# The last rows of w_out on other lanes, and two scalars loaded earlier, in a decode step with attention and a gated MLP

## The chip, the core and the metric

The kernel runs on one core of a Trainium2 chip. A core has five engines that run side by side, each with its own instruction stream: PE (matrix products), DVE (vector operations), ACT (activations and copies), POOL (general small work) and SP, which in this kernel only issues transfers. Sixteen DMA engines move data between device memory and the core's on-chip memory of 128 lanes (partitions). Transfers are issued here from SP and ACT. One transfer is cut into packets, which the DMA engines work off; after its last packet of a transfer each engine reports with a small completion packet of 4 bytes.

The metric is the device time of one execution, in microseconds (us); the median of several runs is taken.

## The reference

One decode step for four sequences: x is 4 x 640 in bf16. The layer norm of x feeds two branches, which are added to x.

```python
def _A_ref(x, k_cache, v_cache, wq, wo):
    B, Sq, D = x.shape                       # 4, 1, 640
    q = (x @ wq) as 32 heads of 128
    scores = einsum('bhqd,bhkd->bhqk', q, k_cache) * Dh ** (-0.5)    # 4096 keys
    o = einsum('bhqk,bhkd->bhqd', softmax(scores), v_cache)
    return o.reshape(B, Sq, Hq * Dh) @ wo

def _B_ref(x, w_in, w_sp, b_sp, w_out):
    z = gelu(x @ w_in)                       # 640 x 1728
    z1, z2 = z[..., :864], layernorm(z[..., 864:])
    g = w_sp * z2 + b_sp                     # w_sp is 1 x 1, b_sp one number
    return (z1 * g) @ w_out                  # 864 x 640

xn = layernorm(x)
return x + _A_ref(xn, ...) + _B_ref(xn, ...)
```

The K and V caches are 4 x 32 x 4096 x 128 in bf16, 134 MB each. With one query row for each head, every byte of them is used once, so nearly all of the 282 MB that the kernel reads are K and V.

## The kernel before

**Units.** The work is cut into 16 units, each of eight heads of one sequence. A unit's K is 4 MB, 128 lanes of 64 KB, and so is its V. K goes through a ring of seven places (`ring`), each a quarter of a unit; V has one whole place (`v_all`). For each quarter of K, DVE multiplies with the query (L537) and folds the halves (L543), and PE adds up the rest (L555). Then come row sums (L569), a maximum, the exponential on ACT (L596), a spreading of the probabilities over heads into `p_m` (L607), and the products with V on PE (L631). After each group of four units the result is multiplied by a part of `wo` (L699).

**Loads.** All large loads are issued by SP, in the order of the list `loads` (L195 to L203). `pump` (L207) goes through it and stops where a place is still taken. At the start stand `wq` (L118), the first quarter of K, the second, `load_w` (`w_in` at L127 and those parts of `w_out` that take one transfer), the other half of K, `load_w_few` (the part of `w_out` that takes several transfers), and unit 1's K. Each transfer reports to one of eight landing semaphores, taken in turn, and the issue that comes eight later on the same semaphore first waits for that landing.

**The MLP.** `w_in` and most of `w_out` lie in `v_all` before the first V comes, the last rows of `w_out` in `p_buf`, the room that later holds `p_m`. The 864 rows of `w_out` are split by `W_OUT` (L62) into parts of n lanes with r rows each. Part one has 128 lanes of five rows, part two 128 lanes of one row, part three 12 lanes of eight rows, 10240 bytes to a lane; part three goes by four transfers, of every fourth lane (three lanes each, L123). The generator `gmlp` (L397) does the products with `w_in` (L404, 14 column groups of the same parts), copies them out of PSUM once for each number of lanes (L414), and does gelu, layer norm and gate on DVE, ACT and PE. Its last step multiplies with `w_out` (L503). Only then is `v_all` free for the first V.

**The scalars.** `wsp_bf` and `bsp_bf`, one number each, are loaded from ACT's queue (L735, L736), after ACT's copy for the first unit's query (L527). POOL casts both to fp32 (L464, L466) for the gate.

**The end.** The last unit's V comes in two halves, the second cut into four transfers, and the last part of `wo` in six (L228, L231). After its last product (L699) ACT copies the sum (L823), and two transfers of 2.5 KB write the output.

Of the kernel before, what the change touches and what calls it, by code (L numbers as in the profile page):

```python
# [10 lines left out]
BF16 = mybir.dt.bfloat16  # L11
# [6 lines left out]
def kernel(  # L18
# [14 lines left out]
    nc = tc.nc  # L33
    P = nc.NUM_PARTITIONS
# [24 lines left out]
    RW = 8  # L59
    QW = HC * Dh  # L60
    RING = 2 * NK - 1
    W_OUT = ((P, 5, 1), (P, 1, 1), (12, 8, 4))  # L62
    assert sum(n * r for n, r, _ in W_OUT) == Fh
    NFC = sum(r for _, r, _ in W_OUT)

    def up(n):
        return -(-n // 256) * 256

    PW = sum(up(r * D) for _, r, _ in W_OUT[1:])
    NOH = D // 2  # L70
# [10 lines left out]
    const = ctx.enter_context(tc.tile_pool(name="const", bufs=1))  # L81
# [17 lines left out]
    ring = places.tile([P, RING, QW], BF16, name="k_ring")  # L99
    x_bf = ring[0:Bsz, 1, 0:D]  # L100
    nc.scalar.dma_start(out=x_bf, in_=A_x.flatten_outer_dims())
    v_all = places.tile([P, NK * QW], BF16, name="v_all")

    wq_sb = v_all[:, 0 : DC * HD].rearrange("p (c n) -> p c n", c=DC)
# [2 lines left out]

    at_v = up(DC * (HD + F))
    w_parts, f0, at_p = [], 0, 0
    for n, r, t in W_OUT:  # L110
        if f0 == 0:
            room = v_all[0:n, at_v : at_v + r * D]
        else:
            room = p_buf[0:n, at_p : at_p + r * D]
            at_p += up(r * D)
        w_parts.append((room.rearrange("p (k n) -> p k n", k=r), f0, n, r, t))
        f0 += n * r
    nc.sync.dma_start(out=wq_sb, in_=A_wq.rearrange("(p c) n -> p c n", c=DC))  # L118

    def load_part(part):  # L120
        w, f0, n, r, t = part
        rows = B_w_out[f0 : f0 + n * r].rearrange("(p k) n -> p k n", k=r)
        for l in range(t):  # L123
            nc.sync.dma_start(out=w[l:n:t], in_=rows[l:n:t])

    def load_w():
        nc.sync.dma_start(out=w_in_sb, in_=B_w_in.rearrange("(p c) n -> p c n", c=DC))  # L127
        for part in w_parts:
            if part[4] == 1:
                load_part(part)  # L130

    def load_w_few():
        for part in w_parts:
            if part[4] > 1:
                load_part(part)

    w_rows = [
# [105 lines left out]
    for e in range(PAR):  # L243
        nc.gpsimd.tensor_copy(
            out=of_row[:, e, :, :, e, :],
            in_=ident[:].rearrange("p (k q) -> p q k", q=QD)[:, 0:Bsz, :, None].to_broadcast(
                [P, Bsz, NQ, LN]
            ),
# [15 lines left out]
    for i in range(NSTAT):  # L264
# [5 lines left out]
        out=rstd[:], in_=mv[:, 1:2], func=ACT.Sqrt, bias=eps_tile[:Bsz], scale=1.0  # L270
# [4 lines left out]
        out=xn_bf,  # L275
# [4 lines left out]
        op1=ALU.mult,  # L280
    )

    wsp_bf = const.tile([1, 1], BF16)
    bsp_bf = const.tile([1, 1], BF16)

    xn_v = xn_bf.rearrange("b (p c) -> b c p", c=DC)
    xnT_ps = ps_m.tile([P, DC, Bsz], BF16, tag="m")
    for c in range(DC):
        nc.tensor.transpose(
            out=xnT_ps[:, c, :], in_=xn_v[:, c, :], identity=ident[:Bsz, :Bsz]  # L290
# [8 lines left out]
    for e in range(PAR):  # L299
        q_ps = ps_pv.tile([P, HG, Dh], FP32, tag="pv", name="q_ps")  # L300
        for c in range(DC):
            for k in range(NQ):
                nc.tensor.matmul(  # L303
                    out=q_ps[k * QD : (k + 1) * QD],
# [5 lines left out]
        rows = const.tile([P, HG, Dh], BF16, name=f"q_rows{e}")  # L310
        nc.vector.tensor_scalar(  # L311
            out=rows[:], in0=q_ps[:], scalar1=scale_qk, scalar2=None, op0=ALU.mult
# [7 lines left out]
        out=hot[:].rearrange("p c h -> p (c h)"),  # L320
        in_=ident[:].rearrange("p (g m) -> p m g", m=QD),
# [6 lines left out]
        out=pick[:, :, Bsz - 1 :].rearrange("p c (k q) -> p c k q", q=QD)[  # L328
            :, :, :, 0 : PAR * Bsz : Bsz
        ],  # L330
        in_=hot[:].rearrange("p c (k e) -> p c k e", e=PAR),
# [4 lines left out]
        out=of_set[:],  # L336
        in_=hot[:].rearrange("p c h -> p (c h)")[:, 0 : PAR * Bsz].rearrange(
            "p (e b) -> p e b", b=Bsz
        ),
# [5 lines left out]
    with nc.allow_low_precision("0 and 1"):  # L345
        nc.vector.tensor_reduce(
            out=own[:],
            in_=ident[:].rearrange("p (h l) -> p h l", h=HT),
# [5 lines left out]
        out=par[:], in_=own[:].rearrange("p (k e) -> p e k", e=PAR), axis=AX.X, op=ALU.add  # L354
# [3 lines left out]
        out=far[:],  # L358
# [13 lines left out]
    for half in range(2):  # L372
        nc.tensor.matmul(
            out=out_ps[OG * half : OG * half + OG, :],
# [15 lines left out]
    by_lanes = []  # L390
    for n, r, _ in W_OUT:
        if by_lanes and by_lanes[-1][0] == n:
# [122 lines left out]
    def stage_q(u):  # L515
        hg, b = divmod(u, Bsz)
        qb_ps = ps_m.tile([P, Dh], FP32, tag="m", name="qbc_ps")
        for e in range(PAR):
            nc.tensor.matmul(  # L519
                out=qb_ps[:],  # L520
                lhsT=of_row[:, e, b].rearrange("p k f l -> p (k f l)"),
                rhs=q_rows[e][:, hg, :],
                start=(e == 0),
                stop=(e == PAR - 1),
            )
        qbcs[u] = small.tile([P, Dh], BF16, name="qbc")
        nc.scalar.copy(out=qbcs[u][:], in_=qb_ps[:])  # L527
# [7 lines left out]
    def product(n):  # L535
        u, r, t = step(n)
        nc.vector.tensor_tensor(  # L537
            out=t, in0=t, in1=qbcs[u][:, None, :].to_broadcast([P, HC, Dh]), op=ALU.mult
        )
# [192 lines left out]
    E = mybir.EngineType  # L732
    with tc.manual_schedule(engines={E.PE, E.DVE, E.Activation, E.SP}):
        stage_q(0)
        nc.scalar.dma_start(out=wsp_bf[:], in_=B_w_sp[0:1, 0:1])  # L735
        nc.scalar.dma_start(out=bsp_bf[:], in_=B_b_sp[0:1].rearrange("(a b) -> a b", a=1))  # L736
        waiting = None
        mlp = gmlp()
        for n in range(NK * NU):
            u, i = divmod(n, NK)  # L740
            product(n)
            if n and n % 2 == 0:
                row_sums(n - 1)
            if i == 0 and u:
                head_max(u - 1)
                if waiting in taken:
                    picked(waiting)
            fold_half(n)
            if n == 1:
                next(mlp)  # L750
                next(mlp)
            if i == 0 and u:
                exps(u - 1)
                if waiting in pvs:
                    take(waiting)
                by_head(u - 1)
            sums(n)
            if i == 0 and u + 1 < NU:
                stage_q(u + 1)
            if i == 0 and waiting is not None:  # L760
                if waiting in taken:
                    picked(waiting)
                if waiting % Bsz == Bsz - 1:
                    group_turn(waiting // Bsz)
                    group_proj(waiting // Bsz)
                waiting = None
            if n == 0:
                next(mlp)
            if n == 1:
                next(mlp)  # L770
                next(mlp)
                next(mlp)
                busy.remove(V)
            if n in turns:
                w = waiting = turns[n]
                if w % Bsz == Bsz - 1:
                    group_den(w // Bsz)
                if w == NU - 3:
                    weighted(w, v_runs[:, 0:NC], more=True)
                    weighted(w, v_runs[:, NC:NR], NG // 2)  # L780
                else:
                    weighted(w, v_runs)
                if i < NK - 1:
                    take(w)
                busy.remove(V)
            pump()
        weighted(NU - 2, v_runs)
        row_sums(NK * NU - 1)
        head_max(NU - 1)
        exps(NU - 1)  # L790
        take(NU - 2)
        by_head(NU - 1)
        den = ps_m.tile([P, NQ, PAR, Bsz], FP32, tag="m", name="den_all")
        nc.tensor.matmul(
            out=den[:],
            lhsT=ones_sq[:],
            rhs=acc[(HG - 1) % NACC][:, :, 0 : PAR * Bsz],
            start=True,
            stop=True,
        )  # L800
        rden = small.tile([P, NQ, PAR, Bsz], FP32, name="rden_all")
        nc.vector.reciprocal(out=rden[:], in_=den[:])
        picked(NU - 2)
        u, b = NU - 1, Bsz - 1
        weighted(u, v_ends[0])
        take(u)
        pick_last(u, more=True)
        for c in range(NC):
            nc.tensor.matmul(  # L809
                out=o_last[0][:, :, :, b],  # L810
                lhsT=v_ends[1][:, c, :],
                rhs=p_m[:, u % 2, NG // 2 + c // CB, c % CB, :].rearrange("p (k e) -> p k e", e=PAR),
                start=False,
                stop=(c == NC - 1),
            )
        o_n = small.tile([P, NQ, PAR, Bsz], BF16, name="o_n_last")
        nc.vector.tensor_tensor(out=o_n[:], in0=o_last[0][:], in1=rden[:], op=ALU.mult)  # L817
        gr[HG - 1] = [o_n[:, h // PAR, h % PAR, :] for h in range(HT)]
        group_proj(HG - 1)

        res = v_all[:, 0:NOH]
        out_v = out.flatten_outer_dims()
        nc.scalar.copy(out=res[0 : OG + Bsz], in_=out_ps[0 : OG + Bsz])  # L823
        nc.scalar.dma_start(out=out_v[:, 0:NOH], in_=res[0:Bsz])
        nc.sync.dma_start(out=out_v[:, NOH:D], in_=res[OG : OG + Bsz])
# [30 lines left out]
```

## Time and profile before

| | |
|---|---|
| median of 3 runs | 661.95 us (661.85 to 662.0) |
| profiled execution | 662.09 us, its span 660.2 us |
| read from device memory | 282.24 MB, 428 GB/s over the span |
| busy in the span | DVE 522.6 us (79%), PE 317.0 us (48%), ACT 29.9 us, POOL 10.1 us |
| DMA, SP's queue (q1) | 8192 packets, 99.1% of the time of 16 engines |
| granted clock of PE | 0.692 |

The span goes from the first to the last instruction of the profiled execution; the rest of its time lies outside. A row of the page's slices has one digit for each fortieth of the span, the busy share in tenths. In a list of instruction groups stand line, engine, operation, shapes and number, then the busy time, the mean of one in ns, and the engine's idle time ahead of them with what ended it. The rows of a wait list have the time in all, the number of waits and the longest. The list of transfers gives the size of each and the median time from issue to landing. "SPq" and "ACTq" are an engine's instruction queue, where transfers are issued and waits are held.

### The profile page before, as it was taken

How to read it: one execution, taken by the hardware profiler on the slowest of the kernel's cores; microseconds unless marked ns; L12 is line 12 of the kernel's file. 1: busy time of each engine (PE TensorE's matmuls, PEld its weight loads, DVE VectorE, ACT ScalarE, POOL GpSimd, SP SyncE). 2: the span in 40 equal slices, each digit the busy share in tenths (PEclk: the TensorE clock that was granted, in tenths of full speed). 3: DMA queues.
4: the chain of work that ended last, by engine and by line, in shares of the span. 5: the costliest groups of instructions: out<-in, count | busy, mean ns of one | idle time of the engine just before them, and what ended most of it. 6: DMA issues, size and time to landing. Idle time of an engine off the chain costs nothing.

```text
span 660.2 us, 4777 instructions
## 1 busy us (share of the span) xinstructions
PE 317.0 (48%) x2083; PEld 136.3 (21%) x2083; DVE 522.6 (79%) x276; ACT 29.9 (5%) x73; POOL 10.1 (2%) x20
## 2 busy tenths in 40 slices
PE   0574372526427363452636336263452534737367
PEld 0231121212213121120212112121120211212124
DVE  1767978959597795969959598695969969999950
ACT  0020000000000000000000000000000000000000
POOL 2300000000000000000000000000000000000000
PEclk9757676766767676585767768676685867676785
DMA  9999999999999999999999999999999999999997
GB/s 369 433 461 434 417 441 434 433 437 438 421 445 426 437 430 441 437 422 433 434 441 441 418 437 441 430 441 421 434 441 437 426 421 445 422 427 436 449 409 284
DMA packets 8232, 282.55 MB, mean 428 GB/s; under 512 B 892, under 2 KB 2184, under 8 KB 2568
## 3 DMA queue, kind: packets, MB, share of 16 engines
q1 hardware_dynamic: 8192, 282.25, 99.1%
q8 instruction: 16, 0.26, 0.1%
q10 hardware_dynamic: 20, 0.01, 0.0%
q14 instruction: 4, 0.03, 0.0%
HBM read 282.24 MB, written 0.01 MB: 428 GB/s over the span
## 4 chain that ended last, share of the span: by engine, by line
DMA 62%; DVE 28%; PE 8%; issue 1%; ACT 0%; DVEq 0%
DMA k_ring<-in_A_k_cache_dram 53%; DVE k_ring L537 14%; DVE k_ring L543 7%; PE s_ps L555 6%; DMA v_all<-in_A_v_cache_dram 4%; DMA k_ring<-in_A_wo_dram 3%; DVE s_sb L569 3%; DMA v_all<-in_A_wq_dram 2%; DVE p_m L607 1%; DVE m L578 1%; PE q_ps L303 1%; PE pv L631 1%; PE out_ps L699 1%; DVE p_m L678 1%; DVE mf L580 1%
## 5 line engine op out<-in xcount | busy, mean ns | idle before, releaser
L537 DVE TENSOR_TENSOR k_ring<-k_ring,qbc 128x8192 bf16<-128x8192 bf16 x64 | 282.9, 4420 | 88.5 <-DMA k_ring<-in_A_k_cache_dram 87.9
L555 PE MATMUL s_ps<-k_ring,ident 128*128 128x512 bf16 x512 | 202.2, 566 | 313.8 <-DVE k_ring L543 313.7
L555 PEld LDWEIGHTS <-ident 128*128 128x128 bf16 x512 | 64.0, 130 | 430.0 <-issue 245.4
L543 DVE TENSOR_TENSOR k_ring<-k_ring 128x4096 bf16<-128x4096 bf16 x64 | 145.9, 2280 | 1.1
L631 PE MATMUL pv<-v_all,p_m 128*32 128x512 bf16 x960 | 62.5, 419 | 0.0
L569 DVE TENSOR_REDUCE s_sb<-s_ps 128x128 f32<-128x1024 f32 x32 | 39.0, 1218 | 3.7 <-PE s_ps L555 3.7
L607 DVE TENSOR_TENSOR p_m<-p_c,own 128x2048 bf16<-128x2048 bf16 x16 | 36.6, 2285 | 0.7 <-ACT p_c L596 0.7
L631 PEld LDWEIGHTS <-p_m 128*32 128x32 bf16 x992 | 26.6, 106 | 42.5 <-issue 23.3
L596 ACT ACTIVATE p_c<-s_sb,nm 128x256 bf16<-128x256 f32 x16 | 8.1, 508 | 342.9 <-DVE nm L588 342.9
L662 PEld LDWEIGHTS o_ps<-o_rows,pick 128*128 128x128 f32 x96 | 20.4, 294 | 4.3 <-issue 3.3
L662 PE MATMUL o_ps<-o_rows,pick 128*128 128x128 f32 x96 | 19.1, 367 | 0.0
L643 ACT COPY o_rows<-pv 128x512 f32<-128x512 f32 x16 | 9.4, 586 | 165.7 <-PE pv L631 165.7
L311 DVE TENSOR_SCALAR q_rows<-q_ps 128x512 bf16<-128x512 f32 x2 | 1.4, 692 | 12.8 <-PE q_ps L303 12.8
L817 DVE TENSOR_TENSOR o_n_last<-o_last,rden_all 128x32 bf16<-128x32 f32 x1 | 0.2, 192 | 12.2 <-PE o_last L809 12.2
L303 PE MATMUL q_ps<-v_all,xnT 128*32 128x512 bf16 x40 | 4.5, 630 | 9.3 <-DMA v_all<-in_A_wq_dram 9.3
L527 ACT CAST qbc<-qbc_ps 128x128 bf16<-128x128 f32 x16 | 4.3, 266 | 97.6 <-PE qbc_ps L519 97.6
L578 DVE TENSOR_REDUCE m<-s_sb 128x1 f32<-128x256 f32 x16 | 6.7, 420 | 0.5
L519 PE MATMUL qbc_ps<-q_rows,of_row 128*128 128x128 bf16 x32 | 6.0, 276 | 0.6 <-DVE q_rows L311 0.6
L519 PEld LDWEIGHTS <-of_row 128*128 128x128 bf16 x32 | 4.1, 132 | 8.1 <-issue 7.4
L716 PE MATMUL o_last<-hot,o_rows 128*128 128x8 f32 x32 | 4.9, 279 | 0.7 <-ACT o_rows L643 0.7
L716 PEld LDWEIGHTS o_last<-hot,o_rows 128*128 128x128 f32 x32 | 4.8, 226 | 1.8 <-ACT o_rows L643 1.6
L699 PE MATMUL out_ps<-k_ring,p_m 128*4 128x320 bf16 x48 | 4.0, 309 | 2.1 <-DVE p_m L691 2.1
(87 smaller groups left out, 81.4 us busy)
## 6 DMA issues: line engine op xcount, KB each, us to landing
k_ring<-in_A_k_cache_dram SPq DMA_DIRECT2D x5, 4096.0 KB, 27.2
v_all<-in_A_v_cache_dram SPq DMA_DIRECT2D x2, 4096.0 KB, 28.2
v_all<-in_A_wq_dram SPq DMA_DIRECT2D x1, 5120.0 KB, 15.4
k_ring<-in_A_k_cache_dram SPq DMA_DIRECT2D x2, 2048.0 KB
k_ring<-in_A_v_cache_dram SPq DMA_DIRECT2D x1, 4096.0 KB
k_ring<-in_A_wo_dram SPq DMA_DIRECT2D x3, 1280.0 KB, 20.6
v_all<-in_B_w_in_dram SPq DMA_DIRECT2D x1, 2160.0 KB
k_ring<-in_A_v_cache_dram SPq DMA_DIRECT2D x1, 2048.0 KB
```

Source lines behind the costliest of these rows:

```text
L303: nc.tensor.matmul(out=q_ps[k * QD : (k + 1) * QD], lhsT=xnT[:, c, :], rhs=wq_v[:, c, k, e], start=(c == 0), stop=(c == DC - 1),)
L519: nc.tensor.matmul(out=qb_ps[:], lhsT=of_row[:, e, b].rearrange("p k f l -> p (k f l)"), rhs=q_rows[e][:, hg, :], start=(e == 0), stop=(e ...
L537: nc.vector.tensor_tensor(out=t, in0=t, in1=qbcs[u][:, None, :].to_broadcast([P, HC, Dh]), op=ALU.mult)
L543: nc.vector.tensor_tensor(out=t[:, :, 0:HD2], in0=t[:, :, 0:HD2], in1=t[:, :, HD2:Dh], op=ALU.add)
L555: nc.tensor.matmul(out=s, lhsT=ident[:], rhs=t[:, :, g * RW : (g + 1) * RW], start=(g == 0), stop=(g == m - 1),)
L569: nc.vector.tensor_reduce(out=scores[u][:].rearrange("p (r c) -> p r c", r=NK)[:, lo : hi + 1 : hi - lo], in_=sums_ps.pop(n // 2)[:], axis ...
L578: nc.vector.tensor_reduce(out=m1[:], in_=scores[u][:], axis=AX.X, op=ALU.max)
L607: nc.vector.tensor_tensor(out=p_m[:, u % 2], in0=p_c.pop(u)[:].rearrange("p (g c) -> p g c", c=CB)[:, :, :, None].to_broadcast([P, NG, CB, HT]
L631: nc.tensor.matmul(out=pvs[u][cg * QD : (cg + 1) * QD, :], lhsT=p_m[:, u % 2, g0 + n].rearrange("p c h -> p (c h)"), rhs=v_at[:, n * CB : ...
L662: nc.tensor.matmul(out=gr[hg][:], lhsT=pick[:, c, Bsz - 1 - b : P + Bsz - 1 - b], rhs=o[:, c, :], start=(b == 0 and c == 0), stop=(b == Bs ...
L699: nc.tensor.matmul(out=out_sum(half), lhsT=o, rhs=wo_sb[:, n, half * NOH : (half + 1) * NOH], start=False, stop=(hg == HG - 1 and n == HT ...
L716: nc.tensor.matmul(out=o_last[0][:, :, :, u % Bsz], lhsT=o[:, c, :], rhs=hot[:, c, :].rearrange("p (k e) -> p k e", e=PAR), start=(c == 0) ...
```

## The change

`W_OUT` now says of each part which lanes go together in how many transfers. Part one is as before. Part two is 32 lanes of one row, in one transfer. Part three is 24 lanes of eight rows: the first 18 lanes by three transfers of every third lane (six lanes each), the last 6 by two transfers of every second lane (three lanes each). The number of column groups stays 14, and the bytes of `w_out` are the same. The loads of `wsp_bf` and `bsp_bf` stand right behind that of x, ahead of every other transfer of ACT.

```diff
-    W_OUT = ((P, 5, 1), (P, 1, 1), (12, 8, 4))
+    W_OUT = ((P, 5, ((P, 1),)), (32, 1, ((32, 1),)), (24, 8, ((18, 3), (6, 2))))
...
     nc.scalar.dma_start(out=x_bf, in_=A_x.flatten_outer_dims())
+    wsp_bf = const.tile([1, 1], BF16)
+    bsp_bf = const.tile([1, 1], BF16)
+    nc.scalar.dma_start(out=wsp_bf[:], in_=B_w_sp[0:1, 0:1])
+    nc.scalar.dma_start(out=bsp_bf[:], in_=B_b_sp[0:1].rearrange("(a b) -> a b", a=1))
...
     def load_part(part):
-        w, f0, n, r, t = part
+        w, f0, n, r, cuts = part
         rows = B_w_out[f0 : f0 + n * r].rearrange("(p k) n -> p k n", k=r)
-        for l in range(t):
-            nc.sync.dma_start(out=w[l:n:t], in_=rows[l:n:t])
+        l0 = 0
+        for lanes, t in cuts:
+            for l in range(l0, l0 + t):
+                nc.sync.dma_start(out=w[l : l0 + lanes : t], in_=rows[l : l0 + lanes : t])
+            l0 += lanes
...
         for part in w_parts:
-            if part[4] == 1:
+            if len(part[4]) == 1:
                 load_part(part)
...
         for part in w_parts:
-            if part[4] > 1:
+            if len(part[4]) > 1:
                 load_part(part)
...
     with tc.manual_schedule(engines={E.PE, E.DVE, E.Activation, E.SP}):
         stage_q(0)
-        nc.scalar.dma_start(out=wsp_bf[:], in_=B_w_sp[0:1, 0:1])
-        nc.scalar.dma_start(out=bsp_bf[:], in_=B_b_sp[0:1].rearrange("(a b) -> a b", a=1))
```

More of the change, by code (lines that the diff above doesn't have):

```diff
@@ L109 @@
     w_parts, f0, at_p = [], 0, 0
-    for n, r, t in W_OUT:
+    for n, r, cuts in W_OUT:
         if f0 == 0:
@@ L115 @@
             at_p += up(r * D)
-        w_parts.append((room.rearrange("p (k n) -> p k n", k=r), f0, n, r, t))
+        w_parts.append((room.rearrange("p (k n) -> p k n", k=r), f0, n, r, cuts))
         f0 += n * r
@@ L281 @@
     )
-    wsp_bf = const.tile([1, 1], BF16)
-    bsp_bf = const.tile([1, 1], BF16)
     xn_v = xn_bf.rearrange("b (p c) -> b c p", c=DC)
```

## The prediction

> **What bounds the kernel now.** I read the page's slices first, then its DMA lines, the stage windows, the chain, the queue's waits and the timeline of SP, and last the trace's single DMA packets and landing events.
>
> ```profile
> DVE  1767978959597795969959598695969969999950
> DMA  9999999999999999999999999999999999999997
> DMA packets 8232, 282.55 MB, mean 428 GB/s; under 512 B 892, under 2 KB 2184, under 8 KB 2568
> q1 hardware_dynamic: 8192, 282.25, 99.1%
> q8 instruction: 16, 0.26, 0.1%
> DMA 62%; DVE 28%; PE 8%; issue 1%; ACT 0%; DVEq 0%
> ```
>
> The DMA row is 9 in every slice but the last, and SP's queue (q1) holds 99.1% of all engine time. The chain gives only 62% to DMA, since it goes through the DVE and PE steps that let SP issue the next load; an issue that comes while older transfers still run costs nothing. Whether one ever comes too late is in the windows (PE, PEld, DVE, ACT and POOL busy, granted clock, DMA share, GB/s):
>
> ```profile
> 10.00:30.00 20.00, 6.14 (x46) 2.20 (x46) 9.40 (x5) 0.27 (x1) 3.02 (x2) 0.87 1.00 427
> 30.00:45.00 15.00, 11.40 (x164) 7.02 (x164) 9.56 (x22) 4.63 (x7) 3.08 (x1) 0.61 1.08 461
> 45.00:65.00 20.00, 10.57 (x44) 3.55 (x40) 15.94 (x6) 0.25 (x1) 0.00 (x0) 0.65 1.00 433
> 200.00:600.00 400.00, 189.48 (x1124) 79.61 (x1123) 334.25 (x162) 14.54 (x40) 0.00 (x0) 0.68 1.00 433
> 640.00:655.00 15.00, 10.86 (x182) 7.98 (x183) 1.77 (x4) 0.70 (x2) 0.00 (x0) 0.58 0.96 394
> ```
>
> A share of 1.00 (1.08 where packets overlap) says that the DMA engines are never without a packet between 10 and 640 us. The packet records agree: sixteen packets or more are in flight for 651 of the 660.2 us. So no issue time matters, and the end is set by the engine whose own packets add up to most. The sixteen landing events of the last `wo` transfer show who that is: the first engine lands at 653.79 us, the last at 656.92, with eight engines in the last 0.61 us (lags behind the first of 2.52 to 3.13 us). Following packets from engine to engine, those eight carry the q8 instruction blocks: each block sets its engine back by some 1.4 us, mostly two blocks to an engine. The three engines that carry `w_out`'s twelve-lane part are not among them; they end with lags of 1.47 to 1.7 us. The other five lie between 0 and 2.0 us. After the last landing only this is left:
>
> ```profile
> 656.11 0.71 PEld L699 LDWEIGHTS <-o_n_last 128*4 128x4 bf16 x7 [0.47 <-issue]
> 657.43 0.42 ACT L823 CAST v_all<-out_ps 36x320 bf16<-36x320 f32 x1 [9.36 <-PE out_ps L699]
> 657.87 0.30 SPq L825 DMA_DIRECT2D out_dram<-v_all  x1
> ```
>
> The profiled execution took 662.09 us (span 660.2, 1.9 outside it); the median shown is 661.95. I sum against 662.09 and move the median by the same difference.
>
> **The change, part by part.**
>
> *128 rows become 32 rows.* The 160 KB transfer of one row per lane gives every engine 8 packets of 1280 bytes; 32 rows give every engine 2. A 1280-byte packet takes 55 ns and the next starts 3 to 4 ns before its end, so each engine sheds 6 x 51.5 ns = 0.31 us. This holds for the eight last engines too, and is on the path: their last landing goes from 656.92 to 656.61. Bounds: zero, if those packets hid behind another engine, against 6 x 55 ns = 0.33. I take 0.31, the packet row itself.
>
> *12 lanes become 24.* A lane is one packet of 10240 bytes, 385 ns; with its 9 ns completion packet and the overlaps, 387 ns. Before, four three-lane transfers put four such packets on each of three engines (twelve packets between 41.6 and 43.4 us, four to an engine). After, three six-lane transfers and two three-lane ones have 24 packets. No row shows a six-lane transfer, so I bound it: on six engines, the same three would carry 5 and three more 3; on three engines alone, each would carry 3 x 2 + 2 = 8. In the first case the old three gain 0.39 - 0.31 = 0.08 us (lag up to 1.76) and the new three gain 3 x 0.387 - 0.31 = 0.85. If these are light engines they reach at most 1.96 + 0.85 = 2.81, just under the heavy ones' new 3.13 - 0.31 = 2.82: nothing on the path. If they are heavy, the end moves by +0.85. In the second case the old three reach 1.7 + 4 x 0.387 - 0.31 = 2.9, and the end falls by only 0.2. I take six engines, all of them light: a three-lane transfer gives each lane its own engine, and the eight engines with instruction blocks leave out all of the first three, which fits a set of neighbours further on better than a scattered one.
> The Trainium skill (page "DMA: Bandwidth & Descriptors", section "Why a DMA increments its semaphore by 16 and not by 1") says that such a transfer takes as many engines, up to 16, as divide its outermost size, starting at the lowest-numbered. By it six lanes mean six engines, among them the former three; the trace agrees for three lanes (three engines, four packets each), and by the rule the sum would be the one I take.
>
> *One more small transfer on SP.* Issues there take 0.33 us each and sit under full DMA engines. SP waits, at each issue, for the landing of the transfer eight issues earlier; the rows of before are
>
> ```profile
> SPq L124 <- DMA k_ring<-in_A_k_cache_dram: 8.5, 2, 4.5
> SPq L124 <- DMA bsp_bf<-in_B_b_sp_dram: 0.6, 1, 0.6
> 20.95 7.95 SPq L124 DMA_DIRECT2D p_m<-in_B_w_out_dram  x4
> 32.04 0.34 SPq L164 DMA_DIRECT2D k_ring<-in_A_k_cache_dram  x1
> v_all<-in_B_w_out_dram SPq DMA_DIRECT2D x1, 800.0 KB, 29.5
> ```
>
> With `wsp` and `bsp` moved ahead, the instruction order of the changed kernel has the small transfers wait for `wsp`, `bsp`, the first two K quarters and `w_in`, and the next whole K load for the first part of `w_out`, which lands at 3.40 + 29.5 = 32.9 us. So that K load is issued at about 32.9 instead of 32.04. Queued behind it is the first V load. Cover: the two K quarters ahead of it, which land between 41.7 and 43.3 us, some 8.8 us later. If that cover were gone, 0.9 us. All later waits shift by one semaphore with the same transfer behind them.
> The last small packets end near 43.5 us and land by 43.9; their reader, the L503 products on `p_m`, starts at 46.04. Cover 2.1 us.
>
> *A third copy at L414.* The lane groups become 128, 32 and 24, so DVE does three copies for two: 0.33/2 = 0.17 us more, in a stage where it waits for PE before (1.32 us at 36.68) and for ACT after (2.06 us at 43.98). At worst yT and the first V load (46.29) come 0.17 us later; the K load ahead keeps the engines busy until 60.8. Nothing. PE has as many products as before.
>
> *`wsp` and `bsp` right behind x.* They leave ACT's queue at 21.66 and 21.92 (0.23 and 0.46 us) for about 1.3, where ACT has nothing until its table load at 4.20: nothing, and 0.7 us less behind the first `qbc`. POOL casts them at about 5.5 instead of 26.98 (1.76 and 4.39 us under DVE's products), off every path. On the one engine that carries a single element each, such a packet takes 9 ns; but at the start, with nothing in flight, one of x's packets took 960 ns. So 0.02 to 1.92 us on that engine, if both pay in full. If it is one of the three with small lanes, its lag goes from 1.76 to 3.68 at worst, and the end to +0.55 us. I take 0.02, as three of x's four packets took 53 to 60 ns.
>
> Sum: -0.31 on the path, all else hidden: 662.09 - 0.31 = 661.78 for the profiled execution, 661.64 for the median (0.05% less).
>
> **The rivals.**
>
> A. *Nothing visible.* The lags of the heavy engines come from when instruction blocks arrive (0.6 us between the eight), and another of them, or a newly loaded one at 2.81, sets the end. For: the two limits, 2.81 and 2.82, touch. Against: every engine sheds the same 0.31. Time 661.95.
>
> B. *The three newly loaded engines are among the heavy ones.* Then up to 3.13 + 0.85 sets the end: +0.85, 662.8, slower than before. It decides as soon as one engine with a lag over 2.3 us gets three of the packets. For: the trace does not number the engines. Against: a set of eight neighbours that leaves out the first three leaves the next ones out too, unless it starts right there.
>
> C. *The early single elements hold up their engine*: up to +0.55, 662.5. Against: three of four start packets were short.
>
> D. *A small transfer costs its engines a fixed time, not only its packets.* Upward from rows: the only transfers that show such a surcharge are the instruction blocks (1.4 us for 0.6 us of packet). Even 0.8 us on each of five transfers instead of four leaves the three engines at 1.76 + 0.8 = 2.6, no effect; if all engines stood idle for one, +0.8 - 0.31 = 662.4. Against: successive small packets overlap by 3 ns.
> The Trainium skill speaks against the change here (same page, "Rules for kernel authors": transfers under 64 KB pay mostly overhead; its section "Anatomy of one DMA", on POOL's path, has about 2.0 us fixed for each). My estimate from that for one more transfer in everybody's path is 663.6; the twelve packets without a gap between them do not show it.
>
> E. *A better balance than I see*: the mean lag is 1.99 us, so a perfect spread would end 1.14 us earlier, 660.8. The change moves only 0.31 off the heavy engines, so this needs luck in where instruction blocks fall.
>
> **How the numbers follow.** A measurement of this kernel tells about 0.2% (1.3 us) from no change. Forecast 0.55, A 0.19, B 0.09, C 0.06, D 0.06, E 0.05. All but the far end of D (and a mix of B with a third instruction block) lie within 0.2%: faster 0.03, same 0.91, slower 0.06. The predicted time is 661.65. Leaving out half of E and D, the range is 661.0 to 662.8; the forecast's own is 661.4 to 661.9.
>
> **What would show it.** Right: q1 with 8192 - 96 + 12 + 12 = 8120 packets, 2100 under 2 KB; six engines with 10240-byte packets near 42 us, three with five and three with three; the K load of 32.04 at 32.9 with the DMA share still 1.00; the last landing near 656.6, L823's cast near 657.1, a span of 659.9. Wrong: a share under 1.00 in 30:65 us (late issues), a first packet on one engine that starts a microsecond late (C), or a last landing after 657.5 on an engine that carries three small packets (B).

## The result, and the profile after

The changed kernel takes 664.29 us (median of 5, 664.06 to 664.99), the one before 661.95 (661.85 to 662.01) on the same chip: a ratio of 1.0037, 95% interval 1.0025 to 1.0048. It is slower by 2.3 us, outside the range of 661.0 to 662.8. The profiled execution took 664.49 us, its span 662.6.

The page of the changed kernel, its slices and DMA lines:

```profile
DMA  9999999999999999999999999999999999999996
DMA packets 8160, 282.55 MB, mean 426 GB/s; under 512 B 904, under 2 KB 2100, under 8 KB 2484
q1 hardware_dynamic: 8120, 282.25, 99.0%
q8 instruction: 16, 0.26, 0.1%
```

The packets are what was counted ahead: 8120 on SP's queue, 2100 under 2 KB. The bytes are the same and the DMA engines are still never idle. So the loss is not in how many packets there were in all. The stage windows around the small transfers show where, of the kernel before:

```profile
31.00:41.00 10.00, 7.41 (x152) 5.49 (x150) 6.93 (x15) 3.42 (x5) 2.08 (x1) 0.67 1.07 455
41.00:47.00 6.00, 4.99 (x26) 1.88 (x26) 3.62 (x8) 1.45 (x2) 0.00 (x0) 0.50 1.16 501
80.00:600.00 520.00, 246.73 (x1448) 103.51 (x1448) 433.30 (x206) 18.91 (x52) 0.00 (x0) 0.68 1.00 433
```

and of the changed kernel:

```profile
31.00:41.00 10.00, 7.48 (x145) 6.76 (x143) 5.97 (x11) 2.64 (x4) 0.00 (x0) 0.50 1.04 440
41.00:47.00 6.00, 4.85 (x16) 1.78 (x18) 2.45 (x12) 2.00 (x4) 0.00 (x0) 0.50 1.10 369
80.00:600.00 520.00, 244.24 (x1448) 102.11 (x1448) 434.12 (x207) 18.81 (x52) 0.00 (x0) 0.69 1.00 433
```

The last two columns are the DMA share and GB/s, counted by the packets that start in the window. Between 41 and 47 us the share is over 1 in both, but 369 GB/s stand against 501: the engines are full and move less. From 80 us on the two rows agree.

The packet records of this stretch say which packets. Before, all twelve small packets of `w_out` take 385 ns and the first sixteen packets of the first whole K load (128 of 64 KB, one for each lane, so that a unit's K is 8 MB and not 4), on every engine, 2418 ns. In the changed kernel the first five small packets take 385 ns, the other 19 442 to 947 ns (3.9 us too much in all), and the first sixteen K packets 2784 to 3912 ns: 17.6 us too much, a mean of 1.1 us for each engine and at least 0.37 us, whether it carries small packets or not. I call this the stretch.

The landing events of the last half of `wo` show the second loss. Before, the sixteen engines land between 653.79 and 656.92 us, the last but one at 656.73. After, fifteen engines land by 657.92 and the last one alone at 659.39. So 657.92 - 656.73 = 1.19 us are common to all and the last engine stands another 1.47 - 0.19 = 1.28 us behind. Behind it the end is as before, L826 being the old L823:

```profile
659.89 0.42 ACT L826 CAST v_all<-out_ps 36x320 bf16<-36x320 f32 x1 [9.22 <-PE out_ps L704]
660.33 0.29 SPq L828 DMA_DIRECT2D out_dram<-v_all  x1
```

SP's timeline and its waits in the changed kernel, for the steps that were called hidden:

```profile
16.75 15.14 SPq L130 DMA_DIRECT2D p_m<-in_B_w_out_dram  x5
33.41 0.35 SPq L171 DMA_DIRECT2D k_ring<-in_A_k_cache_dram  x1
48.26 0.33 SPq L182 DMA_DIRECT2D v_all<-in_A_v_cache_dram  x1
```

```profile
SPq L171 <- DMA v_all<-in_B_w_out_dram: 1.4, 1, 1.4
```

The K load waits for the first part of `w_out` as foreseen and is issued at 33.41 (32.04 before), and the first V load at 48.26 (46.29). Both come while older transfers run.

### The profile page after: what moved, and what is told of

Same layout as the page of the kernel before. It is cut to its first block, busy times and chain, and to the rows that moved or that the text cites. A ratio compares the mean times of both kernels' runs of the same rounds, so it can differ in the third digit from the quotient of the medians.

```text
span 662.6 us, 4781 instructions
## 1 busy us (share of the span) xinstructions
PE 316.5 (48%) x2083; PEld 136.8 (21%) x2083; DVE 522.7 (79%) x277; ACT 29.8 (4%) x73; POOL 4.3 (1%) x20
## 3 DMA queue, kind: packets, MB, share of 16 engines
q1 hardware_dynamic: 8120, 282.25, 99.0%
## 4 chain that ended last, share of the span: by engine, by line
DMA 64%; DVE 27%; PE 7%; issue 1%; SPq 0%; ACT 0%; DVEq 0%
DMA k_ring<-in_A_k_cache_dram 53%; DVE k_ring L542 13%; DVE k_ring L548 6%; PE s_ps L560 6%; DMA v_all<-in_B_w_out_dram 5%; DMA v_all<-in_A_v_cache_dram 4%; DMA k_ring<-in_A_wo_dram 4%; DVE s_sb L574 3%; DVE p_m L612 1%; DVE m L583 1%; PE pv L636 1%; PE out_ps L704 1%; DVE p_m L683 1%; DVE mf L585 1%; DVE nm L593 0%
## 5 line engine op out<-in xcount | busy, mean ns | idle before, releaser
L667 PEld LDWEIGHTS o_ps<-o_rows,pick 128*128 128x128 f32 x96 | 18.9, 273 | 4.1 <-issue 3.2
L667 PE MATMUL o_ps<-o_rows,pick 128*128 128x128 f32 x96 | 17.7, 346 | 0.0
L409 PE MATMUL zT<-xnT,v_all 128*24 128x4 bf16 (+2 forms) x140 | 6.4, 182 | 0.0
L409 PEld LDWEIGHTS <-v_all 128*24 128x24 bf16 (+2 forms) x140 | 6.4, 135 | 0.0
L636 PE MATMUL pv<-k_ring,p_m 128*32 128x512 bf16 x32 | 3.6, 630 | 3.8 <-DMA k_ring<-in_A_v_cache_dram 3.8
```

What stands on the lines that cost most here:

```text
L409: nc.tensor.matmul(out=zT[0:n, t, k, :], lhsT=w_t[:, c, f : f + (n - 1) * r + 1 : r], rhs=xnT[:, c, 0:Bsz], start=(c == 0), stop=(c == DC ...
L636: nc.tensor.matmul(out=pvs[u][cg * QD : (cg + 1) * QD, :], lhsT=p_m[:, u % 2, g0 + n].rearrange("p c h -> p (c h)"), rhs=v_at[:, n * CB : ...
L667: nc.tensor.matmul(out=gr[hg][:], lhsT=pick[:, c, Bsz - 1 - b : P + Bsz - 1 - b], rhs=o[:, c, :], start=(b == 0 and c == 0), stop=(b == Bs ...
```

## The experiments

All are timed against the kernel before on the same chip, at 661.95 to 662.00 us. "Small packets" are those of 10240 bytes near 42 us; the K excess is the time beyond 2418 ns of the first sixteen 64 KB packets, summed.

### Scalars or lanes

The scalars alone: the loads of `wsp` and `bsp` behind that of x in the kernel before.

> The kernel before with the two scalars loaded right behind x and nothing else. Theory S (lanes: the stretched packets at 41 to 47 us come from which lanes the small transfers write): 661.95 +- 0.2, every 10240-byte packet near 42 us takes 385 ns, the first whole K load's packets 2418 ns. Theory T (scalars: the early single elements hold up their engine or the queue): 663 to 664.3.

The lanes alone: the changed kernel with those two loads back behind `stage_q(0)`.

> The changed kernel with the two scalar loads put back where they were. Theory S: 664.3 +- 0.4, stretched packets as in the changed kernel. Theory T: 661.6 to 662.2, no stretched packets.

The scalars alone take 662.01 us, ratio 0.9999 (0.999 to 1.0009), with no small packet over 385 ns and no K excess. The lanes alone take 664.42, ratio 1.0034 (1.002 to 1.0048), with 4.3 us of excess on the small packets and a K excess of 17.1 us. The windows of 41 to 47 us, first the scalars alone, then the lanes alone:

```profile
41.00:47.00 6.00, 4.99 (x36) 2.13 (x34) 3.58 (x8) 1.46 (x3) 0.00 (x0) 0.76 1.16 501
```

```profile
41.00:47.00 6.00, 4.88 (x22) 1.79 (x22) 2.85 (x12) 2.19 (x4) 0.00 (x0) 0.69 1.08 363
```

501 GB/s as before, and 363, near the 369 of the changed kernel: all of the loss is in the lanes.

### Which lanes a transfer takes

Four six-lane transfers of every fourth lane, run twice:

```diff
-    W_OUT = (..., (24, 8, ((18, 3), (6, 2))))
+    W_OUT = (..., (24, 8, ((24, 4),)))
```

Here and in the other kernels whose last part has a single pair (lanes, transfers), `load_w` and `load_w_few` go by the number of transfers in that pair; these lines are left out of the cuts.

> The changed kernel with the 24 lanes in four transfers of every fourth lane (0, 4, ... 20), six lanes each. Theory S (two engines of one transfer write into the same group of four lanes, which here never happens): no stretched packets, the next K load ends 1.2 us earlier than in the changed kernel on the first engine; six engines carry four small packets, one of them an engine with instruction blocks, so the last landing stands some 1.2 us behind that engine's old place: 662.7 to 663.3. Rival R (six engines reading w_out at once is what stretches, whatever the lanes): stretched packets as in the changed kernel, 664.3 to 665.

> The six-by-four kernel once more, for a profile of its faster kind: 662.8 to 663.1, the last landing about 1 us behind that of before on one engine alone, the other fifteen not later than before; in the slower kind (667 to 669) all K packets from 31 us on take 220 ns more for every 32 KB.

In the kernel before, three neighbouring lanes a transfer instead of every fourth:

```diff
-            nc.sync.dma_start(out=w[l:n:t], in_=rows[l:n:t])
+            nc.sync.dma_start(out=w[l * n // t : (l + 1) * n // t], in_=rows[l * n // t : (l + 1) * n // t])
```

> The kernel before with its 12 lanes in four transfers of three neighbouring lanes (0 to 2, 3 to 5, ...) instead of every fourth lane: same bytes, same three engines, same number of packets. Theory S: small packets over 385 ns and a first K load that ends 0.3 to 1.3 us later on every engine: 662.3 to 663.3. Rival R: no stretch, 661.95 +- 0.2.

The six-by-four kernel came out in two groups: 662.82 to 663.6 us in 10 of 16 executions, and 667.7 to 669.0 in the other six (on the second group see the end). The second run's profile is of the first group (662.92). In it every small packet takes 385 ns and there is no K excess, with the same six engines, 24 lanes and 24 packets; its window of 41 to 47 us is

```profile
41.00:47.00 6.00, 4.91 (x24) 1.83 (x26) 2.98 (x12) 2.17 (x4) 0.00 (x0) 0.71 1.15 494
```

So six engines reading `w_out` at once do not stretch anything, and the 1 us by which this kernel is still slower than the one before is the other loss: fifteen engines land their last packet by 656.78 (656.73 before) and one at 657.84.

The neighbouring lanes stretched, but mostly themselves: the twelve small packets have 1.5 us of excess, up to 0.54 each, the first sixteen K packets 1.2 us in all. The time is 662.00, ratio 1.0 (0.999 to 1.0009). The expectation of 662.3 to 663.3 missed. That the excess fell on the engines of the small packets, which have room, fits the landings, though no row names an engine: before, three engines landed their last packet 1.47 to 1.68 us behind the first, here one does so at 1.69 and the next follow at 2.48 and 2.57, still ahead of the last at 3.25. Its window moves as much as that of before:

```profile
41.00:47.00 6.00, 4.40 (x35) 1.79 (x33) 3.86 (x7) 1.45 (x2) 0.00 (x0) 0.78 1.20 501
```

### Lanes written or rows read

With the step between lanes, the step between the rows read had changed too. Two kernels separate them, with the rows of `w_out` permuted over the lanes.

```diff
+        if n == 24:
+            src = [slice(0, 18, 3), slice(1, 18, 3), slice(2, 18, 3), slice(18, 24)]
+            for l in range(4):
+                nc.sync.dma_start(out=w[l:n:4], in_=rows[src[l]])
```

> The changed kernel, its 24 lanes written by four six-lane transfers of every fourth lane, but with the source rows taken in the changed kernel's groups (every third block of eight rows, then the last six), so that rows of w_out stand on other lanes and the result is permuted. Theory S (the lanes written cause the stretch): no stretched packets, 662.8 to 663.2 as the six-by-four kernel's faster runs. Rival H (which rows are read at the same time causes it): first whole K load stretched by over 1 us on every engine, 664.3 to 665.

```diff
+        if n == 24:
+            for l in range(3):
+                nc.sync.dma_start(out=w[l:18:3], in_=rows[l:n:4])
+            for l in range(2):
+                nc.sync.dma_start(out=w[18 + l : n : 2], in_=rows[3 + 12 * l : 12 + 12 * l : 4])
```

> The reverse: the changed kernel's lanes (every third, then every second), with source rows taken every fourth block; again the rows of w_out are permuted over the lanes. Theory S: stretch as in the changed kernel, 664.3 +- 0.4. Rival H: no stretch, three small packets on the loaded engine, 662.4 to 662.9.

Lanes in fours with the changed kernel's rows: 662.53 to 663.62 us in 8 of 10 executions (667.2 and 669.2 in the others), as the six-by-four kernel. Lanes in threes with rows in fours: 664.21 to 665.38, median 664.77, ratio 1.0041 (1.0026 to 1.0056), just above what was expected, with 4.2 us of excess on the small packets and a K excess of 14.9 us. What is written decides, not what is read. Both profiles also fell on executions with longer K packets from about 32 us on, ahead of the small ones (median of the K half 1396 and 1361 ns against 1213; see the end), so a part of each excess is of that kind. The two kinds look different: in the first kernel's profile (669.16 us) all small packets take 433 to 435 ns and the first sixteen K packets 2782 to 2785, in the second's they scatter from 426 to 976 and from 2739 to 4118.

### The sixth engine, and the stretch without it

Five lanes to a transfer instead of six, with 64 rows in part two:

```diff
-    W_OUT = (..., (32, 1, ((32, 1),)), (24, 8, ((18, 3), (6, 2))))
+    W_OUT = (..., (64, 1, ((64, 1),)), (20, 8, ((20, 4),)))
```

> The changed kernel with 64 lanes of one row and 20 lanes of eight, the 20 by four transfers of every fourth lane (five engines). Every engine has four packets of 1280 bytes less than before (0.21 us), five engines have four small packets each. If the one engine with instruction blocks is the sixth: 661.6 to 661.9, last landing near 656.7. If it is among the first five: 662.9 to 663.2. Theory S: no stretched packets.

```diff
-    W_OUT = (..., (64, 1, ((64, 1),)), (20, 8, ((20, 4),)))
+    W_OUT = (..., (64, 1, ((64, 1),)), (20, 8, ((15, 3), (5, 1))))
```

> The five-by-four kernel (64 lanes of one row, 20 of eight, 662.06) with its 20 lanes written by three transfers of every third lane (15 lanes) and one of the five next to one another: the same five engines and four packets each, so nothing on the sixth, but two engines write into one group of four lanes. Theory S: small packets over 385 ns, all engines' first K packets stretched by about 1 us, 662.9 to 663.4. If the loaded sixth engine were the whole loss of the changed kernel and the stretch hidden: 662.0 +- 0.2.

Five by four takes 662.06 us, ratio 1.0 (0.999 to 1.001). No engine stands alone behind the others: the last lands at 657.10, the last but one at 657.01. With six lanes one engine was 1.07 us behind the rest; without the sixth lane the kernel is back at the time of before. In all six profiles with six-lane transfers the last engine lands 1.03 to 1.53 us behind the last but one, in the two with five lanes 0.09 and 0.12. So it is the sixth engine that cannot take the packets. Its gain of 0.21 us did not come, though.

With the lanes in threes and the same five engines, the kernel takes 663.22, ratio 1.0018 (1.0009 to 1.0028): 1.16 us more than five by four. The small packets have 2.3 us of excess, the K packets 12.5; the last two engines land at 657.81 and 657.92, so all are late together. The windows, five by four and then five by three:

```profile
41.00:47.00 6.00, 4.99 (x26) 1.87 (x28) 3.31 (x12) 2.08 (x4) 0.00 (x0) 0.76 1.14 493
```

```profile
41.00:47.00 6.00, 4.99 (x33) 2.10 (x34) 3.83 (x12) 1.75 (x3) 0.00 (x0) 0.81 1.09 400
```

Each loss has now been seen alone: the stretch 1.16 us, the sixth engine 0.9 to 1.0 us (a median of 662.96 for six by four in its first group, with four packets to that engine, against 662.06 and 662.00).

### Two lanes of one group, or any lane of another engine

The Trainium skill (page "DMA: Bandwidth & Descriptors", section "The descriptor swizzle") says that in a transfer over 128 lanes each engine writes eight lanes in two groups of four neighbours: the first engine lanes 0 to 3 and 32 to 35, the second 4 to 7 and 36 to 39, and so on. No row of a profile tells an engine's lanes, but the runs agree: with lanes in fours, a small transfer's first engine would write lanes 0 to 3, its second 4 to 7, as in K, and nothing stretches; with any other step something does. Two kernels ask whether two small packets have to meet in one group. The first writes two lanes, four apart, and one lane alone, in turn:

```diff
-            nc.sync.dma_start(out=w[l:n:t], in_=rows[l:n:t])
+            nc.sync.dma_start(out=w[l + t : n : t], in_=rows[l + t : n : t])
+            nc.sync.dma_start(out=w[l : l + 1], in_=rows[l : l + 1])
```

> The kernel before, its twelve lanes written by four transfers of two lanes (4 and 8, 5 and 9, ...) and four of one lane (0, 1, 2, 3). In the two-lane transfers the first engine writes the group of four that the second one writes in large transfers, the second engine that of the third; no two of one transfer share a group. If it takes two small packets in one group to stretch: all twelve small packets 385 ns. If it is enough that an engine writes another engine's group, whose owner writes K there: the packets of lanes 4 to 11 take 420 to 800 ns. The time says little: 661.9 to 662.6, since the first engine carries eight of the packets.

```diff
-    W_OUT = (..., (24, 8, ((18, 3), (6, 2))))
+    W_OUT = (..., (24, 8, ((24, 6),)))
```

> The changed kernel's parts (32 lanes of one row, 24 of eight), the 24 by six transfers of every sixth lane (0, 6, 12, 18; 1, 7, 13, 19; ...): four engines with six small packets each. Here the four lanes of a transfer lie in four different groups of four, but two of the four engines write a group that another engine fills in large transfers; in the third and later transfers the pattern shifts but never pairs. If pairs in one transfer make the stretch: all small packets 385 ns, first K packets 2418 ns, 661.6 to 662.3 (each engine 0.31 us less, the fourth engine 2.3 us more on a light lag), or 667 to 669 in the slower kind that 32-lane kernels have shown. If writing another engine's group is enough: small packets at 420 ns and more, K packets stretched by about 1 us on all engines, 662.8 to 663.5.

The first did not answer it. Its eight transfers made SP wait so long that the queue ran dry, which the expectation had not seen; its SP timeline and its window:

```profile
33.36 0.57 SPq L127 DMA_DIRECT2D p_m<-in_B_w_out_dram  x1
43.60 0.22 SPq L128 DMA_DIRECT2D p_m<-in_B_w_out_dram  x1
43.95 0.35 SPq L168 DMA_DIRECT2D k_ring<-in_A_k_cache_dram  x1
```

```profile
41.00:47.00 6.00, 4.99 (x23) 1.89 (x23) 3.27 (x9) 1.75 (x3) 0.00 (x0) 0.50 0.59 206
```

Its eighth small transfer, eight issues behind the K half, waits until that has landed (43.6 us), and the K load is issued at 43.95, when most engines have had nothing since about 41.6. The kernel takes 666.27 us in its one execution, 666.27 - 661.96 = 4.3 us more: a wait of the kind that was called hidden in the prediction, with its cover gone. Little K was written while eleven of its twelve small packets went through at 385 ns, so they say nothing about lanes beside K. Its first sixteen K packets, which start after the gap on engines that had been empty, have 10.0 us of excess although only the last small packet still runs beside them: long K packets alone do not prove misplaced lanes, and the comparison has to be between queues that stay full, as in the other runs.

The second has six transfers of four lanes, of which no two lie in one group. It takes 665.34 us (4 executions, ratio 1.0054, 1.0037 to 1.0071), where 662.8 to 663.5 was expected for a stretch, with 3.3 us of excess on the small packets and a K excess of 13.8 us; the window shows 352 GB/s:

```profile
41.00:47.00 6.00, 4.99 (x22) 1.89 (x20) 2.75 (x12) 1.93 (x4) 0.00 (x0) 0.64 1.04 352
```

So no pair within a transfer is needed. By the Trainium skill's map (the same section), it would be enough that lanes are not the writing engine's own. This is argued, not shown: no row tells an engine's lanes, and no run has every fourth lane on shifted engines beside a full queue of K, so the step of four itself may be what counts. That its time is still above that of the changed kernel has two visible parts, the stretch and four engines with six packets each; they were not separated.

## Why the prediction was wrong

**What bounds the kernel** held: the DMA engines are never idle and the slowest one's landing sets the end, in every run but that of eight small transfers, where the queue ran dry.

**The price of a small packet was the step that failed.** The prediction took 387 ns for each of the 24, from the twelve of before, and nothing for their neighbours. That row was measured with lanes in fours. With lanes in threes and twos 19 of the 24 took longer, and the sixteen engines lost 1.1 us each, in the mean, on the K packets beside them. Neither the bounds (six engines or three) nor a rival had a packet that slows other engines. The nearest was rival D's far end, all engines held up once (662.4), but its cause, a fixed cost for each transfer, is refuted: four six-lane transfers in fours, and four five-lane ones, went through at 385 ns a packet. The Trainium skill's rule against small transfers, weighed there, would have charged these as well.

**"All of them light" was wrong by one engine.** Rival B (0.09) named the mechanism and its price, +0.85, and said that one heavy engine among the three newly loaded ones is enough; the forecast took all three for light. One is heavy: taking the sixth lane out takes the lone late engine away. It stands 1.28 us further behind than the last engine did before. Three packets at 387 ns less six small ones account for 0.85; the rest, some 0.4 us, no run separates. That the sixth engine carries instruction blocks rests on following packets from engine to engine in the six-by-four kernel and the changed one (there with blocks at 287 and 642 us); neighbours a few ns apart can be confused in that.

**The 0.31 us that every engine sheds** were counted right (8 packets to 2) and did not show at the end. In the six-by-four kernel the last landing but one is at 656.78, not 656.4; in five by four, 0.21 us were expected and the time is that of before. In its profile the packets of the K half after 30 us have 0.16 us of excess for each engine in the mean, nearly all of it in the first sixteen packets behind the 64 rows (1222 to 1561 ns against 1213), which would eat most of it there; for the six-by-four kernel (0.02 us) that does not hold, and where the rest goes is open.

**The hidden steps** were hidden. The K load's issue was predicted for 32.9 and came at 33.41; the copies at L414 (L419 in the changed file) take 0.39 us for three against 0.33 for two, where 0.17 more was expected. The first V load came 2.0 us later, not 0.17, mostly because the 140 products with `w_in` took 6.38 us instead of 4.61, where the prediction counted only that their number stays. The granted clock from 31 to 41 us, 0.50 instead of 0.67, is not the reason: the scalars alone, with the old lane groups, took 4.66 us at 0.50, and four by six, with the new groups, 6.34 at 0.70. The 80 products of the small groups take 4.0 us with 24 columns and 2.3 with 12; why is open. The V load still met a full queue. The scalars cost nothing, as the first experiment shows, and rival C is out. Their single elements did not wait for a first packet of 960 ns: they went at 5.9 and 8.9 us, each behind a packet of `wq`, 9 ns long, so the first cast came at 7.8, not 5.5.

**Two readings of the working** were off without touching the forecast. The mean lag in E is 1.93 us by the sixteen landings, not 1.99, so a perfect spread would end 1.2 us earlier. The instruction blocks in D have packets of 0.88 to 0.97 us, not 0.6.

**The sum** by what was measured: 1.19 us common to all engines and 1.28 on the last one make 2.47 at the last landing, of which 2.40 appear in the profiled times (664.49 - 662.09).

None of the kernels tried is faster than the one before; five by four equals it, and so does the kernel before with neighbouring lanes.

## What to carry to other kernels

Where all DMA engines are always busy, count packet time for each engine, instruction fetches included, and put extra rows only on engines that end early. A row's price belongs to its pattern: a transfer of few lanes ran beside large ones at its own packets' time when it took every fourth lane, and slowed all sixteen engines when it took every second, third or sixth. Before a transfer is cut into more pieces, count eight issues back on the queue to see what its successor will wait for.

## What the hardware showed that was not expected

Small writes of 245 KB to few lanes slowed engines that carried none of them: in the changed kernel the first K packet of every engine took 15 to 62% longer, 17.6 us in all, beside 24 small packets that would take 0.4 us each.

Two kernels with 32 rows in part two and lanes in fours (six by four in both runs, and the one with permuted rows) had executions of 667 to 669 us beside those of 663, 8 in 26; neither the kernel before nor five by four with 64 rows had one, nor the four kernels with 32 rows and other steps (18 executions). The profiles of two such executions show the packets of K and V longer by 12 to 18% on all engines, from about 32 us to 80 us (for 32 KB mostly 1436 and 1396 against 1213 ns, for 64 KB from 54 us on 2714 and 2789 against 2418), and full speed from then on. The window of 47 to 80 us in the first six-by-four run:

```profile
47.00:80.00 33.00, 11.33 (x42) 3.87 (x39) 25.75 (x13) 0.66 (x3) 0.00 (x0) 0.61 1.00 384
```

and in the second run's execution of 662.92 us:

```profile
47.00:80.00 33.00, 11.57 (x46) 4.03 (x45) 30.28 (x14) 0.87 (x3) 0.00 (x0) 0.62 1.00 432
```

384 GB/s stand against 432, both at a DMA share of 1.00. This slowing begins ahead of the small packets, right behind the 32 rows. The kernel with lanes in threes and rows in fours has it too in its profile (665.28 us; two of its four executions took about a microsecond more than the other two), but there it ends by 48 us, behind the stretched small packets. What starts it and what ends it is open.
